# Six edits to a three-part kernel: products to GpSimd, stash copies in runs, one expert's order, weight loads on another queue

## The chip, the core and the metric

One Trainium2 chip, of which the kernel uses one core. The metric is the device time of one execution in microseconds (us). A core has TensorE (PE in the profile; its weight loads are PEld), VectorE (DVE), ScalarE (ACT), GpSimd (POOL) and SyncE (SP, here a queue for transfers only). Each engine works through its own list of instructions in order, and waits on semaphores where an instruction needs another engine's result or a transfer.

## What is computed

The reference, cut to its core. `q`, `k`, `v`, `a_re` and `a_im` are 4 x 8 x 768 x 48; `x` is 3072 x 384; there are 8 experts of 384 x 1024 x 384, and a last dense layer of 384 x 2048 x 384.

```python
# 1. a linear recurrence with a complex decay, per batch and head
scale = np.minimum(mag, 0.999) / (mag + 1e-06)
for t in range(S):
    S_re, S_im = ar * S_re - ai * S_im + kv[t], ar * S_im + ai * S_re
    y[:, :, t] = np.einsum('bhd,bhde->bhe', q[:, :, t], S_re)
# 2. of the tokens with x @ w_skip > 0 each goes to one expert
e_idx = np.argmax(xc @ w_gate, axis=1)
y[mask] = gate_w[mask, None] * (np.maximum(xc[mask] @ w1[e], 0.0) @ w2[e])
out[do_compute] = xc + y
# 3. a dense layer with a leaky ReLU
h = x @ w_in
return np.maximum(0.01 * h, h) @ w_out
```

## The kernel before

The four batches are worked in two units of two. For a unit there are these steps.

The **row side** (`attention_rows`) lays 128 rows (chunk, batch, head) on the partitions and walks through 96 time steps in blocks of 8 (at the ends fewer). Per step VectorE makes `t` (four products of the running decay product `P` with the block's normalised decay `a`) and the next `P` (two sums). Around this chain stand, per block: the normalising of `a` (`norm_pre`, `norm`: tiles `nsq`, `nr`, `nrr`, `a`) and the scaling of q and k (`scaled_pre`, `scaled`: tiles `psq`, `pg`, `pu`, `kq`). `scaled` multiplies q and k by the real and by the imaginary half of `P`; in unit 0 into `qr` and `kr`. In unit 0 `added` lets TensorE add the two squares in a bank of PSUM (tile `ad`), and `turned` transposes `qr` and `kr`, four time steps at a time, into PSUM (tile `qkps`), from where ScalarE copies them into the two `stash` tiles, which stay in SBUF and are laid out (chunk, batch and head, time). In unit 0 all of it is emitted from a table of due times (`timed`), with VectorE, ScalarE and TensorE held to that written order; `gate_products` (tiles `gv`, `gvT`, `gps`) is spread between.

The **chunk side** (`attention_chunks`) does the recurrence over eight chunks of 96 steps as matmuls. The row side of unit 1, called `behind`, runs in its gaps: `budget` lets it go on for so many microseconds of VectorE at each yield. It writes to DRAM (tile `kqd`) and not to the stash.

Then **routing**, and for the tokens of unit 0 the eight **experts** (`experts`): `gathers` fetches 128 rows for each (tile `xg`, an indirect transfer per expert), `columns` transposes them (tile `tp__`, copied by ScalarE to `xT__`), `first` and `second` are the two layers (tiles `hps`, `hh`, `yps`, `xo`), and the rows are scattered back into `xd`. The weights of unit 0's experts lie in the stash tiles in fp32; those of experts 4 to 7 are loaded by `fetch` into the place of an earlier expert's as soon as that is used. After the first layer of expert 3 `swap` lets the second stash tile go, and `convert` starts to bring `w_in` in: a 64-bit load (tile `raw`, two buffers), three VectorE instructions that put together an fp32 number (tile `cst`), a ScalarE copy to fp16 and one more VectorE instruction for the rest (tile `m2w`), 16 pieces in all. `feed` shares VectorE's budget between `behind` and this, in turns (class `share`; class `first_of` runs one to its end before the next). `BG_EXPERT` = 2.0 us are given at each of the four yields of `first`, up to expert `LASTE`.

Then the **dense** layer for unit 0's 1536 tokens: `Dense.load` (tile `xr`) reads what the experts scattered; in the first 512 tokens `w_out` is converted as well. Then unit 1: chunk side, experts (whose weights are converted to fp16 pairs), dense layer.

Which transfer stands on which queue is set in the code: nearly all on SP's, the weights of unit 0's experts on ScalarE's.

```python
    for j in range(n + 1):
        if j:
            A.activation(hi[cut(j - 1)], t[j - 1], AF.Copy, scale=scale)
        if j < n:
            r = pool.tile([128] + shape + [2], I32, tag="raw", name="raw")
            nc.sync.dma_start(...)                      # L805
```

Of the kernel before, what the change touches and what calls it, by code (L numbers as in the profile page):

```python
# [48 lines left out]
BG_START = 1.5  # L49
BG_CHUNK = 0.3  # L50
BG_ROUTE = 12.0
BG_EXPERT, LASTE = 2.0, 6
BG_DENSE = (1, 1.5, 1.5)
BG_WOUT = 0.3
BG_WSTART, BG_WEIGHT = 4.0, 0.35
# [11 lines left out]
SUM_NORM = (0, 1, 2)  # L67
SUM_SCALED = (12, 13)
MIRROR = (0, 1)
GUARD_G = (10, 11, 13)  # L70
MIRROR_G = (11, 12, 13)
LISTS = dict(sp=(0, 1), tp=(2, 3, 7), yps=(4,), ups=(5,), tr=(6,), bk=(7,))
DEEP = {"kqt": 3, "vt": 3, "qT": 3}
LISTSA = dict(sp=(0, 1), yps=(2,), ups=(3,), tr=(4, 5, 6), bk=(7,))
# [4 lines left out]
def moe_attention_kernel(ctx, tc, q, k, v, a_re, a_im, w_skip, w_gate, w1, w2, w_in, w_out, out,  # L79
# [70 lines left out]
    def rows3(x):  # L150
        return x.rearrange("(k p) f -> p k f", p=128)


    def attention_rows(ui, ep, blks, sum_pe, queue, store, stash=None, more=None):
# [124 lines left out]
        def scaled(i):  # L279
            P = Ps.pop(i)  # L280
            kq2 = ins.pop(("k", i))
            u = tl("pu", i)
            if stash:
                kq = [tl(x, i, (), (2,)) for x in ("kr", "qr")]
            else:
                kq = tl("kq", i, (), (2, 2))
                kq = [kq[:, :, a] for a in range(2)] + [kq]
            if stash:
                V.tensor_tensor(kq[1][:, :, 0], kq2[:, 1], P[:, :, 0], ALU.mult)
                yield cost(i)  # L290
                V.tensor_tensor(kq[1][:, :, 1], kq2[:, 1], P[:, :, 1], ALU.mult)
            else:
                V.tensor_tensor(kq[1], both(kq2[:, 1], i), P, ALU.mult)
            yield cost(i, 2)
            n2, g0 = pre["k", i]
            V.tensor_tensor(u, n2, g0, ALU.mult)
            yield cost(i)
            V.scalar_tensor_tensor(u, u, 2.0, g0, ALU.subtract, ALU.mult)
            yield cost(i)
            V.scalar_tensor_tensor(kq2[:, 0], kq2[:, 0], -1.0, u, ALU.mult, ALU.mult)  # L300
            yield cost(i)
            if stash:
                V.tensor_tensor(kq[0][:, :, 0], kq2[:, 0], P[:, :, 0], ALU.mult)
                yield cost(i)
                V.tensor_tensor(kq[0][:, :, 1], kq2[:, 0], P[:, :, 1], ALU.mult)
            else:
                V.tensor_tensor(kq[0], both(kq2[:, 0], i), P, ALU.mult)
            if i + 2 < nb:
                load_kq(i + 2)
            if stash:  # L310
                turns.append(turned(i, kq))
            else:
                queue.dma_start(kqd[t0s[i]:t0s[i] + blks[i]].rearrange("t r a d -> r t (a d)"),
                                kq[2].rearrange("r t a c d -> r t (a c d)"))
            yield cost(i, 2)

        def turned(i, kq):

            for g in range(0, blks[i], 4):
                m = min(4, blks[i] - g)  # L320
                for a in range(2):
                    p = ps.tile([2 * D, m, R], F32, tag="qk", name="qkps")
                    for j in range(m):
                        T.transpose(p[:, j, :], kq[a][:, g + j].rearrange("p c d -> p (c d)"), ident)
                    t = t0s[i] + g
                    lags.append((stash[a][:2 * D, :, :, t:t + m].rearrange("p c b t -> p t (c b)"), p))
                    if len(lags) > 1:
                        A.activation(*lags.pop(0), AF.Copy)
                    yield
# [461 lines left out]
    def convert(pool, src, hi, lo, scale, cut, shape, n):  # L791

        raw, t = {}, {}
        el = 1
        for d in shape:
            el *= d
        cost = (70 + 1.04 * el) / 1e3
        for j in range(n + 1):  # L800
            if j:
                A.activation(hi[cut(j - 1)], t[j - 1], AF.Copy, scale=scale)
            if j < n:
                r = pool.tile([128] + shape + [2], I32, tag="raw", name="raw")
                nc.sync.dma_start(r.rearrange("p k f w -> p k (f w)").bitcast(I64), rows3(src)[cut(j)])  # L805
                t[j] = pool.tile([128] + shape, I32, tag="cst", name="cst")
                V.tensor_scalar(t[j], r[:, :, :, 1], 0x07FFFFFF, 3, ALU.bitwise_and, ALU.logical_shift_left)
                yield 0.6 * cost
                V.scalar_tensor_tensor(t[j], r[:, :, :, 1], -0x40000000, t[j], ALU.bitwise_and, ALU.bitwise_or)
                yield cost  # L810
                V.scalar_tensor_tensor(t[j], r[:, :, :, 0], 29, t[j], ALU.logical_shift_right, ALU.bitwise_or)
                t[j] = t[j].bitcast(F32)
                yield cost
            else:
                yield 0.0
            if j:
                V.scalar_tensor_tensor(lo[cut(j - 1)], t[j - 1], scale, hi[cut(j - 1)], ALU.mult, ALU.subtract)
                yield cost
# [20 lines left out]
    class Experts:  # L839
# [2 lines left out]
            self.ui, self.whole, self.place = ui, whole, place  # L842
            self.w, self.xg, self.xt, self.h, self.slots, self.made = {}, {}, {}, {}, [], 0

        def weights(self, e, layer, half):

            src, k, m = ((w1[e], 3, F1), (w2[e], 8, DM))[layer]
            t = self.w[e, layer] = self.place(e, layer).rearrange("p (k m) -> p k m", k=k)
            c = (al, al, slice(half * m // 2, (half + 1) * m // 2)) if layer == 0 else \
                (al, slice(half * k // 2, (half + 1) * k // 2))  # L850
            nc.scalar.dma_start(t[c], rows3(src)[c])

        def part(self, i):

# [96 lines left out]
    class Dense:  # L951
# [4 lines left out]
        def load(self):  # L956
            self.xr = self.xp.tile([128, 4, DM], F32, tag="xr", name="xr", bufs=1)
            nc.sync.dma_start(self.xr, xd[self.ui][self.t * TN:(self.t + 1) * TN, :]
                              .rearrange("(s p) c -> p s c", p=128))
# [43 lines left out]
    def run(*gens):  # L1003
        for gen in gens:
            for _ in gen:
                pass
# [146 lines left out]

    def experts(ex, behind, us, then={}, mixed=none):

        ex.columns(0)
        for e in range(E):
            gen = none if ex.place else ex.made_to(2 * e + NSLOT, ex.stage)
            if e in (() if ex.place else MIX):
                next(mixed, None)  # L1160

            def go():
                for _ in range(3):
                    next(gen, None)
                budget(behind, us if e < LASTE else 0.0, "VA")

            for _ in ex.first(e):
                go()
            then.get((e, 0), list)()
            if e + 1 < E:  # L1170
                ex.columns(e + 1)
            run(gen)
            ex.second(e)
            then.get((e, 1), list)()
# [35 lines left out]
    def fetch(*which):  # L1210
        def go():
            for e, layer in which:
                for half in range(2):
                    ex.weights(e, layer, half)
        return go

    chunks_and_routing(ck[0], rt, later(BG_START, behind), BG_CHUNK,
# [12 lines left out]
    mlp2 = {}  # L1230

    def swap():
# [4 lines left out]
        for i, (shape, src, scale, cut, part) in enumerate((  # L1237
# [1 line left out]
                ([128, 16, DM], w_out, SWO, cut_rows(16, CVP), [16 // CVP, DM]))):  # L1239
            t = mlp2[i] = [wpm.tile(shape, F16, name=f"m2w{i}{j}") for j in range(2)]  # L1240
            mlp2["conv", i] = convert(cp, src, *t, scale, cut, part, CVP)
        feed.gens.append(mlp2["conv", 0])

    then = {(i // 2, i % 2): fetch((i // 2 + 2, i % 2)) for i in range(8, 12)}
    then.update({(i, 1): fetch((4 + i // 2, i % 2)) for i in range(4)})
# [196 lines left out]
```

## Time and profile before

| | |
|---|---|
| three runs | 951.84, 952.55, 953.05 us; median 952.55 |
| the profiled execution | 956.44 us, of which the span of instructions is 954.0 us |
| busy share of the span | TensorE 88%, VectorE 64%, ScalarE 54%, GpSimd 14% |
| 20 to 151 us | row side of unit 0 |
| 151 to 240 us | chunk side of unit 0 |
| 240 to 381 us | routing and experts of unit 0, conversion of `w_in` |
| 381 to 512 us | dense layer of unit 0 (its first 512 tokens up to 444, with the conversion of `w_out`) |
| 512 to 954 us | unit 1 |

A busy share is an average over stages with different limits, so each stage has to be read by itself. The profile names the line of a helper (L91) for all compute instructions, so tiles tell them apart. "a <-b" is an output and its inputs; a wait is put down to what came last.

### The profile page before, as it was taken

To read this page: it belongs to the slowest core of one execution; us is meant where nothing else is said; L and a number is where in the kernel's file an instruction comes from. 1 tells how busy PE (TensorE), PEld (TensorE's weight loads), DVE (VectorE), ACT (ScalarE), POOL (GpSimd) and SP (SyncE) were. 2 spreads that over 40 slices of the span, in tenths; PEclk is the share of its full clock that TensorE was granted. 3 is DMA by queue.
4 is the path that set the end of the run, shared out by engine and by line. 5 is a ranking of instruction groups with operands and counts; after the bars stand their busy time and mean duration, and the time that the engine had idled before them with its cause. 6 is when DMAs were issued, how large, how long until landed. Compare 5 with 4: busy or idle time off the path is not lost.

```text
span 954.0 us, 17829 instructions
## 1 busy us (share of the span) xinstructions
PE 840.4 (88%) x6674; PEld 584.8 (61%) x6674; DVE 612.4 (64%) x1534; ACT 518.0 (54%) x1065; POOL 137.2 (14%) x168
## 2 busy tenths in 40 slices
PE   1787878899299783999999988999999999999997
PEld 1665667898288572455457978846776645546454
DVE  6978884677788579999961555587577262260430
ACT  4879896676255343654743867655566261350430
POOL 9100022221541012000012111140011000000000
PEclk9979897999599986999999989999999999999999
DMA  5555544898668876445246898242766201000000
GB/s 152 143 152 159 139 114 144 243 290 268 200 206 276 283 271 217 147 134 172 78 156 165 224 234 241 75 162 86 246 201 214 88 1 51 18 1 25 9 10 27
DMA packets 126512, 143.61 MB, mean 151 GB/s; under 512 B 34058, under 2 KB 109514, under 8 KB 126416
## 3 DMA queue, kind: packets, MB, share of 16 engines
q1 hardware_dynamic: 106064, 107.88, 38.5%
q10 hardware_dynamic: 18304, 29.89, 9.6%
q0 software_dynamic: 2048, 4.61, 1.4%
q8 instruction: 54, 0.88, 0.4%
q14 instruction: 42, 0.34, 0.1%
HBM read 115.62 MB, written 28.41 MB: 151 GB/s over the span
## 4 chain that ended last, share of the span: by engine, by line
PE 55%; DVE 16%; DMA 14%; ACT 10%; issue 3%; SPq 1%; ACTq 0%; POOL 0%; DVEq 0%; POOLq 0%
PE ops L91 17%; PE hps L91 13%; PE yps L91 7%; PE sps L91 4%; DVE gg L91 3%; DMA raw<-in_moe_w_in_dram 3%; DVE gl L91 3%; DVE cst L91 2%; PE ad L91 2%; ACT stash L91 2%; PE tps L91 2%; ACT gh L91 2%; DMA kqt<-kqd 2%; PE ups L91 2%; DMA cw<-in_moe_w_dram 2%
## 5 line engine op out<-in xcount | busy, mean ns | idle before, releaser
L91 PE MATMUL hps<-xTh,m2w 128*128 128x512 f16 x576 | 174.1, 381 | 0.6 <-issue 0.3
L91 PEld LDWEIGHTS <-m2w 128*128 128x128 f16 x864 | 84.5, 98 | 100.7 <-issue 3.9
L91 PE MATMUL ops<-m2w,gh 128*128 128x384 f16 x512 | 125.2, 326 | 0.0
L91 PE MATMUL hps<-xTl,m2w 128*128 128x512 f16 x288 | 109.4, 381 | 0.1
L91 DVE TENSOR_TENSOR gg<-hps,gg 128x512 f32<-128x512 f32 x96 | 65.8, 685 | 65.5 <-ACT gg L91 65.1
L91 PE MATMUL ops<-m2w,gl 128*128 128x384 f16 x256 | 83.5, 326 | 0.0
L91 ACT ACTIVATE ot<-ops 128x384 f32<-128x384 f32 x24 | 11.6, 489 | 121.2 <-PE ops L91 121.2
L91 PEld LDWEIGHTS <-gh 128*128 128x128 f16 x512 | 50.1, 98 | 32.7
L91 DVE TENSOR_TENSOR t<-P,a 128x192 f32<-128x192 f32 x190 | 66.8, 352 | 1.3 <-ACT a L91 0.4
L91 PE MATMUL ops<-m2w,stash 128*128 128x384 f16 x384 | 65.3, 326 | 1.8 <-ACT m2w L91 1.8
L91 ACT ACTIVATE gg<-hps 128x512 f32<-128x512 f32 x96 | 56.3, 586 | 17.5 <-PE hps L91 12.4
L91 DVE TENSOR_TENSOR gl<-gg,gh 128x512 f16<-128x512 f32 x64 | 44.2, 690 | 33.6 <-ACT gh L91 33.3
L91 DVE SCALAR_TENSOR_TENSOR w<-cw,w 128x768 f16<-128x768 f32 x64 | 59.8, 953 | 7.7 <-ACT w L91 7.2
L91 ACT ACTIVATE gh<-gg 128x512 f16<-128x512 f32 x64 | 40.3, 630 | 43.2 <-DVE gg L91 42.9
L91 ACT ACTIVATE w<-cw 128x768 f16<-128x768 f32 x64 | 53.0, 844 | 17.9 <-DMA cw<-in_moe_w_dram 15.4
L91 POOL TENSOR_SCALAR_AFFINE_SELECT sc<-sc 96x384 f32<-96x384 f32 x64 | 34.6, 550 | 157.6 <-ACT sc L91 157.2
L91 PEld LDWEIGHTS <-stash 128*128 128x128 f16 x384 | 37.5, 98 | 29.2 <-issue 4.8
L91 POOL DMA_INDIRECT xd<-xo,idx x16 | 25.2, 1574 | 179.9 <-DVE xo L91 166.1
L91 ACT ACTIVATE stash<-qkps 96x512 f32<-96x512 f32 (+1 forms) x50 | 50.0, 1025 | 0.4 <-PE qkps L91 0.4
L91 DVE TENSOR_TENSOR P<-t 128x96 f32<-128x96 f32 x190 | 48.5, 255 | 1.6
L91 PE MATMUL yps<-stash,hh 128*128 128x384 f32 x128 | 44.7, 503 | 3.8 <-ACT hh L91 3.8
L91 ACT ACTIVATE hh<-hps 128x256 f32<-128x256 f32 (+1 forms) x64 | 23.8, 378 | 40.6 <-PE hps L91 28.7
(245 smaller groups left out, 1779.6 us busy)
## 6 DMA issues: line engine op xcount, KB each, us to landing
stash<-in_moe_w_dram ACTq DMA_DIRECT2D x32, 768.0 KB
cw<-in_moe_w_dram SPq DMA_DIRECT2D x64, 384.0 KB
kqt<-kqd SPq DMA_DIRECT2D x16, 576.0 KB
kqd<-kq SPq DMA_DIRECT2D x14, 576.0 KB
vd<-gv SPq DMA_DIRECT2D x32, 192.0 KB
vt<-vd SPq DMA_DIRECT2D x32, 192.0 KB
raw<-in_moe_w_in_dram SPq DMA_DIRECT2D x16, 384.0 KB
raw<-in_moe_w_out_dram SPq DMA_DIRECT2D x16, 384.0 KB
```

The source lines that it names most:

```text
L91: ins = getattr(self.engine, op)(*args, **kw)
```

## The change

It has six parts. The two products of `scaled` with q are made by GpSimd in blocks 0 to 10 of unit 0 (`SCALED_G`), and six smaller instructions of blocks 10, 11 and 13 that GpSimd made (`GUARD_G`, `MIRROR_G`) go back to ScalarE. The copy into the stash runs over four time steps innermost. In `experts` of unit 0 TensorE is held to the written order up to the second expert's transposes. `convert` asks for its next piece one piece ahead, and its first as soon as `swap` runs. `feed` gives the conversion all of VectorE's budget until it is done, and then `behind`; and expert 6 has the budget as well (`LASTE` = 7). `fetch` puts the weights of experts 4 to 7 on SP's queue.

```diff
-BG_EXPERT, LASTE = 2.0, 6
+BG_EXPERT, LASTE = 2.0, 7
...
-GUARD_G = (10, 11, 13)
-MIRROR_G = (11, 12, 13)
+GUARD_G = ()
+MIRROR_G = ()
+SCALED_G = range(11)
...
             if stash:
-                V.tensor_tensor(kq[1][:, :, 0], kq2[:, 1], P[:, :, 0], ALU.mult)
+                X = G if i in SCALED_G else V
+                X.tensor_tensor(kq[1][:, :, 0], kq2[:, 1], P[:, :, 0], ALU.mult)
                 yield cost(i)
-                V.tensor_tensor(kq[1][:, :, 1], kq2[:, 1], P[:, :, 1], ALU.mult)
+                X.tensor_tensor(kq[1][:, :, 1], kq2[:, 1], P[:, :, 1], ALU.mult)
...
-                    lags.append((stash[a][:2 * D, :, :, t:t + m].rearrange("p c b t -> p t (c b)"), p))
+                    lags.append((stash[a][:2 * D, :, :, t:t + m].rearrange("p c b t -> p (c b) t"),
+                                 p.rearrange("p t r -> p r t")))
...
+        def load(j):
+            raw[j] = pool.tile([128] + shape + [2], I32, tag="raw", name="raw")
+            nc.sync.dma_start(raw[j].rearrange("p k f w -> p k (f w)").bitcast(I64), rows3(src)[cut(j)])
+
+        load(0)
+        yield 0.0
         for j in range(n + 1):
+            if j + 1 < n:
+                load(j + 1)
             if j:
                 A.activation(hi[cut(j - 1)], t[j - 1], AF.Copy, scale=scale)
             if j < n:
-                r = pool.tile([128] + shape + [2], I32, tag="raw", name="raw")
-                nc.sync.dma_start(r.rearrange("p k f w -> p k (f w)").bitcast(I64), rows3(src)[cut(j)])
+                r = raw.pop(j)
...
-        def weights(self, e, layer, half):
+        def weights(self, e, layer, half, queue=nc.scalar):
...
-            nc.scalar.dma_start(t[c], rows3(src)[c])
+            queue.dma_start(t[c], rows3(src)[c])
...
+        if ex.place:
+            keep("T")
         ex.columns(0)
         for e in range(E):
...
             if e + 1 < E:
                 ex.columns(e + 1)
+            keep("")
             run(gen)
...
-                    ex.weights(e, layer, half)
+                    ex.weights(e, layer, half, nc.sync)
...
-        feed.gens.append(mlp2["conv", 0])
+        next(mlp2["conv", 0])
+        feed.gens = [first_of([mlp2["conv", 0]] + feed.gens)]
```

VectorE's list in the row side of unit 0, in the middle of a block (`qr<-kq_566` are the two products with q of the block before), first as it was:

```order
L91 TENSOR_TENSOR P<-t_774 128x96
L91 TENSOR_TENSOR qr<-kq_566,P 128x8x48
L91 TENSOR_TENSOR t_787<-P,a_614 128x192
L91 TENSOR_TENSOR qr<-kq_566,P 128x8x48
L91 TENSOR_TENSOR P<-t_787 128x96
L91 TENSOR_TENSOR t_802<-P,a_614 128x192
```

and the same place with the change:

```order
L92 TENSOR_TENSOR P<-t_774 128x96
L92 TENSOR_TENSOR t_787<-P,a_614 128x192
L92 TENSOR_TENSOR P<-t_787 128x96
L92 TENSOR_TENSOR t_802<-P,a_614 128x192
L92 TENSOR_TENSOR P<-t_802 128x96
```

The two products have left VectorE's list, and the chain's rows close up. GpSimd's list with the change, from its last memsets of the start on:

```order
L92 MEMSET gv_153 96x8x16
L92 MEMSET stash 32x12288 x2
L92 TENSOR_TENSOR qr<-kq_109,P 128x4x48 x2
L92 TENSOR_TENSOR qr<-kq_115,P 128x8x48 x2
L92 TENSOR_TENSOR qr<-kq_305,P 128x8x48 x2
```

The products stand there one block after the other, behind the stash's memset.

TensorE's list where the experts of unit 0 begin (`tp__3514` and `tp__3610` are the transposed rows of the first and of the second expert), as it was:

```order
L91 MATMUL bank<-incl_1_3334,ones 96x8
L91 MATMUL tp__3514<-ident,xg_3474 128x128 x3
L91 MATMUL tp__3610<-ident,xg_3479 128x128 x3
L91 MATMUL hps<-xT__3518,stash 128x128 x24
L91 MATMUL yps_3616<-stash,hh 128x384 x8
```

and with the change:

```order
L92 MATMUL bank<-incl_1_3334,ones 96x8
L92 MATMUL tp__3514<-ident,xg_3474 128x128 x3
L92 MATMUL hps<-xT__3518,stash 128x128 x24
L92 MATMUL tp__3610<-ident,xg_3479 128x128 x3
L92 MATMUL yps_3616<-stash,hh 128x384 x8
```

The second expert's transposes went behind the first expert's first layer. SP's queue in the later experts (`raw` are the pieces of `w_in`, `ari` and `kq` belong to `behind`, each with the semaphores that it waits for), as it was:

```order
L805 DMA raw<-in_moe_w_in_dram 128x3x128 [waits DMAHW5_49,DVE_49]
L805 DMA raw<-in_moe_w_in_dram 128x3x128 [waits DMAHW7_49,DVE_49]
L201 DMA ari<-in_a_re_dram 128x1x288 [waits DMAHW0_49,DVE_49,Activation_49]
L202 DMA ari<-in_a_im_dram 128x1x288 [waits DMAHW1_49]
L805 DMA raw<-in_moe_w_in_dram 128x3x128 [waits DMAHW5_49,DMAHW3_49,DVE_49]
```

and with the change (`stash<-in_moe_w_dram` are weights of experts 6 and 7):

```order
L805 DMA raw<-in_moe_w_in_dram 128x3x128 [waits DMAHW5_49,DVE_49]
L805 DMA raw<-in_moe_w_in_dram 128x3x128 [waits DMAHW6_49,DVE_49]
L861 DMA stash<-in_moe_w_dram 128x3x512 [waits DMAHW7_49,PE_49]
L861 DMA stash<-in_moe_w_dram 128x3x512 [waits DMAHW0_49,PE_49]
L805 DMA raw<-in_moe_w_in_dram 128x3x128 [waits DMAHW5_49,DMAHW1_49,DVE_49]
L805 DMA raw<-in_moe_w_in_dram 128x3x128 [waits DMAHW6_49,DMAHW2_49,DVE_49]
L861 DMA stash<-in_moe_w_dram 128x4x384 [waits DMAHW3_49,PE_49]
L861 DMA stash<-in_moe_w_dram 128x4x384 [waits DMAHW4_49,PE_49]
```

Pairs of pieces and pairs of weight loads now take turns on the one queue, and the weights there wait for TensorE.

## Rows read from the trace of the kernel before

**Rows 1.** Windows view, six stretches: busy time (count) per engine, granted clock, DMA share, GB/s.
```profile
20.00:140.00 120.00, 97.52 (x626) 74.18 (x627) 101.67 (x308) 102.48 (x207) 13.58 (x7) 0.89 0.54 145
...
140.00:151.00 11.00, 6.68 (x41) 4.51 (x39) 7.34 (x28) 10.58 (x22) 2.88 (x5) 0.78 0.30 86
...
262.00:307.00 45.00, 45.00 (x269) 36.52 (x268) 36.96 (x107) 24.75 (x64) 14.40 (x9) 0.96 0.73 236
...
307.00:381.00 74.00, 49.98 (x272) 39.29 (x271) 55.05 (x140) 29.47 (x73) 10.74 (x11) 0.84 0.80 259
...
381.00:444.00 63.00, 60.74 (x298) 29.70 (x296) 60.28 (x132) 35.39 (x69) 0.00 (x0) 0.97 0.46 145
...
444.00:512.00 68.00, 68.00 (x386) 37.56 (x384) 49.06 (x130) 32.62 (x75) 6.82 (x9) 1.00 0.49 145
```

**Rows 2.** Chain of waits from 20 to 151 us, its shares by engine and line.
```profile
by line: PE ad L91 17.2%; ACT stash L91 16.6%; issue 8.7%; PE gps L91 8.5%; ACT psq L91 8.5%; ACT gvT L91 5.6%; PE gtps L91 5.6%; ACT nsq L91 4.1%; DMA ari<-in_a_im_dram 3.2%; ACT a L91 3.1%; PE qkps L91 2.9%; ACT gv L91 2.5%; DVE t L91 2.0
```

**Rows 3.** VectorE groups from 20 to 151 us: busy, mean ns, idle before and its releaser.
```profile
L91 DVE TENSOR_TENSOR qr<-kq,P 128x384 f32<-128x384 f32 x20 | 11.0, 551 | 0.0
...
L91 DVE TENSOR_TENSOR pu<-ad,pg 128x384 f32<-128x384 f32 x10 | 5.6, 559 | 14.6 <-ACT pg L91 14.6
```

**Rows 4.** Groups of the whole run, shapes kept apart: ScalarE, VectorE, GpSimd.
```profile
L91 ACT ACTIVATE stash<-qkps 96x512 f32<-96x512 f32 x46 | 47.9, 1062 | 0.0
...
L91 ACT ACTIVATE sT<-stp 96x512 f32<-96x512 f32 x28 | 16.6, 593 | 2.9 <-PE stp L91 2.7
...
L91 DVE TENSOR_REDUCE LG<-xps 96x9 f32<-96x72 f32 x32 | 7.3, 228 | 47.5 <-ACT xrow L91 47.3
...
L91 DVE TENSOR_REDUCE em<-cand 96x14 f32<-96x112 f32 x2 | 0.5, 266 | 0.1
...
L91 POOL TENSOR_SCALAR_AFFINE_SELECT sc<-sc 96x384 f32<-96x384 f32 x64 | 34.6, 550 | 157.6 <-ACT sc L91 157.2
```

**Rows 5.** Timeline: GpSimd beside VectorE: start us, length us, instruction.
```profile
128.16 2.55 POOL L91 TENSOR_SCALAR a<-a 128x192 f32<-128x192 f32 x1 [7.59 <-DVE a L91]
...
128.53 0.25 DVE L91 TENSOR_TENSOR P<-t 128x96 f32<-128x96 f32 x1
...
186.94 1.67 POOL L91 TENSOR_SCALAR_AFFINE_SELECT sc<-sc 96x384 f32<-96x384 f32 x2 [3.12 <-ACT sc L91]
...
188.11 0.61 DVE L91 TENSOR_TENSOR P<-t 128x96 f32<-128x96 f32 x1
```

**Rows 6.** Timeline: one block's last product on VectorE, and TensorE's first transposes of it.
```profile
63.90 0.55 DVE L91 TENSOR_TENSOR qr<-kq,P 128x384 f32<-128x384 f32 x1
...
72.11 0.60 PE L91 MATMUL qkps<-ident,qr 128*96 128x128 f32 x4
```

**Rows 7.** Timeline from 254 to 262 us: the first two experts on TensorE and ScalarE.
```profile
255.11 0.49 ACT L91 ACTIVATE xT__3518<-tp__3514 128x384 f32<-128x384 f32 x1 [1.58 <-PE tp__3514 L91]
...
260.89 0.90 PE L91 MATMUL tp__3610<-ident,xg 128*128 128x128 f32 x3 [5.82 <-DMA xg<-xd,idx]
...
261.58 0.64 PE L91 MATMUL hps<-xT__3518,stash 128*128 128x128 f32 x2
```

**Rows 8.** Chain of waits from 307 to 381 us, in order of time: start us, us, what.
```profile
310.52 9.57 DMA raw<-in_moe_w_in_dram
...
372.00 7.22 DMA xr<-xd
```

**Rows 9.** Waits from 307 to 381 us: us in total, times, longest us.
```profile
DVE cst L91 <- DMA raw<-in_moe_w_in_dram: 13.2, 9, 5.8
...
PE hps L91 <- ACT xT__4174 L91: 4.9, 1, 4.9
...
PE yps L91 <- ACT hh L91: 3.8, 2, 3.0
```

**Rows 10.** Timeline: DMA issues on ScalarE's queue (ACTq).
```profile
317.28 4.03 ACTq L851 DMA_DIRECT2D stash<-in_moe_w_dram  x2
...
334.26 5.35 ACTq L851 DMA_DIRECT2D stash<-in_moe_w_dram  x2
```

## The prediction

> **What bounds the kernel now.** I read the windows view first, stage by stage, then in each stage that the change touches the chain of waits, the groups and the timeline.
>
> In the row side of unit 0 no engine is full, and three are nearly so: from 20 to 140 us TensorE is busy for 97.5 of 120 us, VectorE for 101.7, ScalarE for 102.5 [rows 1]. The chain goes to and fro between TensorE and ScalarE; the stash copies are its largest piece that isn't TensorE's, with 16.6% of 131 us, or 21.7 us [rows 2]. VectorE stands behind them: its idle time before `pu` ends with ScalarE's `pg`, 14.6 us in ten blocks [rows 3]. From 140 to 151 us ScalarE alone is full (10.58 of 11), nearly all of it stash copies [rows 1].
>
> The experts of unit 0 are two stages. From 262 to 307 us TensorE is busy throughout [rows 1], so what starts it earlier counts in full. From 307 to 381 us nothing is full: TensorE is busy for 50.0 of 74 us, VectorE for 55.1 [rows 1]. The chain there goes through transfers: a piece of `w_in` takes 9.57 us from issue to landing, and the rows for the dense layer (`xr`) 7.22 us at the end [rows 8]. VectorE waits 13.2 us for pieces [rows 9].
>
> From 381 to 444 us VectorE is the bound (60.3 of 63 us), from 444 to 512 us TensorE (68 of 68) [rows 1]. What `behind` and the conversions still owe VectorE at 381 is paid in the first of the two; the second has 19 us of VectorE to spare. Unit 1 is not touched.
>
> **The change part by part.**
>
> *Stash copies.* 46 copies of 512 columns take 1.062 us each. Another ScalarE copy of 512 columns out of PSUM, `sT`, takes 0.593 us; it writes its columns one after the other, where the stash copy scatters them singly [rows 4]. The change writes runs of four and reads PSUM with a stride instead. No ScalarE row reads so. The nearest is VectorE's sum `LG`, which reads single numbers 64 apart in PSUM: 72 of them in 0.228 us, against 0.266 us for the 112 of `em` side by side in SBUF [rows 4], which is no sign of a price. So I take 0.6 us a copy, with 1.06 us as the other end (the stride costs in reading what it cost in writing). That is 46 x 0.46 = 21 us less of ScalarE.
>
> *Six instructions back to ScalarE*, of 384 columns at most. Each is less than the 0.593 us of `sT`; at 0.4 us they make +2.4 us.
>
> *Products to GpSimd.* 22 instructions leave VectorE; the 20 of 384 columns in [rows 3] are 11.0 us, two of them stay, and the first block's two are shorter, so some 10.5 us leave it. GpSimd's length for such a product is in no row. Its select over 384 columns, with one input, takes 0.55 us [rows 4]; twice that, 1.1 us, for two inputs is my value. The other end is 2.55 us, which a smaller instruction took while VectorE worked without a gap [rows 5]. Two a block make 2.2 to 5.1 us. They have 8.2 us, from the start of VectorE's last product at 63.90 to TensorE's first transposes of it at 72.11 [rows 6], so they aren't late. If that cover were gone, TensorE and then ScalarE would stop behind them in order. The first block's pair stands behind the stash's memset and is the one place where I leave a delay open.
>
> They do cost VectorE something. In [rows 5] a `P` that starts inside a GpSimd select takes 0.61 us, where the one at 128.53 takes 0.25 us: 0.36 us held by one instruction with one input. With two inputs I take 0.7 us; 22 x 0.7 = 15 us, against 10.5 us taken away. The difference of 5 us goes into VectorE's 18 us of idle time of [rows 1].
>
> The Trainium skill speaks against this edit: by SBUF — State Buffer, "Who interferes with whom", a VectorE instruction with two SBUF inputs and a GpSimd instruction that reads SBUF exclude one another, for the length of one. The row agrees that VectorE is held, for 0.36 us of 0.55. By GPSIMD Engine Reference, "Elementwise — side-by-side cycle accounting", a two-input instruction takes about 2.6 cycles an element, which gives an estimate of 0.83 us for 384; 22 of those would be 18 us on VectorE, and the sum for it +8 us rather than +5. No run so far shows such a product.
>
> What the row side gains by all three: of 21.7 us of copies on the chain 44% goes, 9.5 us. The next chains are near (VectorE at 85% of the stretch plus 5 us, TensorE at 81%), and the six instructions stand on it too. But from 140 to 151 us ScalarE's gain is whole, with seven or eight copies. I take **-8 us**; ends +2.5 (copies no faster) and -14.
>
> *The first expert's order.* The first layer of expert 0 can start when `xT__3518` is copied: 255.11 + 0.49 = 255.6 us. It starts at 261.58, since the second expert's transposes stand ahead and wait until 260.89 for their gather [rows 7]. With the order written out it starts **5.9 us** earlier; the gather is there before the first layer ends. TensorE's 45 full us [rows 1] hand that on to 307.
>
> *Weights on SP's queue, pieces ahead, conversion first.* ScalarE stands 4.03 and 5.35 us at issues of weights [rows 10], and TensorE waits 4.9 and 3.8 us for ScalarE [rows 9]. These 8.7 us go, but TensorE has 24 us of idle time in this stage, so alone they are worth nothing. What counts is VectorE's 19 us of idle time there. 13.2 us of it is waiting for pieces. Asking earlier, in pairs, with the row side to fill in, should take two thirds of that, -9.5 us. I don't take all, since the pieces now queue with the weights on SP, which wait for TensorE. In VectorE's list two more steps of the row side than before stand ahead of the end of `w_out`'s conversion; at 101.7 us for ten blocks of eight steps [rows 1, 3] that is 1.3 us each, +2.5 us. Sum **-7 us**; ends +2.5 and -14. `LASTE` = 7 puts 8 us more of VectorE's work before the last expert's rows; it hides in the same idle time, and if that is gone, `xr` is late by it.
>
> The sum is -8 - 5.9 - 7 = -20.9 us, against the profiled execution's 956.4 us: 935.5. That execution is 3.9 us above the median, so I forecast 931.6, say **932 us**.
>
> **The rivals.**
> 1. *The copies don't get faster.* For it: no row shows a strided read by ScalarE. Against: [rows 4]. The first term goes to +1, the sum to -12: 941 us.
> 2. *The later experts gain nothing.* Pieces at 9.57 us a landing, with the transfers at 0.80 of their time [rows 1, 8], set the conversion's pace, and the 5.9 us are waited away there too. For it: that share, and three things on one queue. Only the row side is left: 944.5 us.
> 3. *SP's queue becomes the chain.* Weights wait on it for TensorE, and pieces behind them. Seven pairs, each with 9.57 us to land and 2.2 us for four VectorE instructions of at most 0.55 us [rows 3, 8], are 82 us from 302: 384 us, and `xr` then at 391 against 379. With the row side's -8 that is +4: 957 us. It decides from a landing of 9.2 us a pair on. Against: with two buffers the landings overlap VectorE's work, and 9.57 us was seen in a crowd only.
> 4. *Slower, by GpSimd.* A product holds VectorE for all of the 2.55 us of [rows 5]: 22 x 2.55 = 56 us, less 10.5 and 18 of idle time, +28; with the other terms +15: 967 us. It decides from 1.9 us a product. Against: at 128.16 GpSimd waited, and the `P` inside its 2.55 us took its usual 0.25 us [rows 5].
> 5. *The terms cancel*, about 951 us.
>
> **How the numbers follow.** Chances: forecast 0.53 (own range 922 to 941), rivals 0.15, 0.17, 0.06, 0.05, 0.04. Faster by more than 0.2% (1.9 us, about what a measurement of this kernel can tell): 0.53 + 0.15 + 0.17 = 0.85; within it 0.04; slower 0.11. The range takes in rivals 1 and 2 and leaves out the rest at both ends: 920 to 950.
>
> **What would show it.** Right: stash copies near 0.6 us; the last of them about 8 us earlier; `hps` of expert 0 right behind its `xT__`, before `tp__` of expert 1; no issue on ScalarE's queue over 1 us in the later experts; less than 5 us of waits for `w_in` pieces; the dense layer's first matmul 18 to 25 us earlier. Wrong: copies still at 1 us; `P` and `t` that take twice their time beside `qr` on GpSimd; TensorE waiting for `qr`; SP's queue standing at weights while VectorE waits for pieces; the gain of the experts given back before 444.

## The result, and the profile after

Four runs took 920.58 to 928.26 us, median 925.17, against 952.58 before: a ratio of 0.9709 (95% interval 0.9663 to 0.9755), by the ratio 27.7 us less. Measured once more the ratio was 0.9719 (0.9689 to 0.9750). The forecast was 932 us, 20.6 us less.

The profiled execution took 920.58 us with a span of 918.9. Set against the profiled one of before, at the points where the stages begin:

| start of | before, us | after, us | earlier by | in this stage |
|---|---|---|---|---|
| chunk side (first `sps`) | 153.55 | 138.69 | 14.9 | 14.9 |
| first layer of expert 0 | 261.58 | 241.39 | 20.2 | 5.3 |
| first `cst` of `w_in` | 308.67 | 289.06 | 19.6 | -0.6 |
| dense layer (first `hps` of `xTh`) | 381.06 | 350.17 | 30.9 | 11.3 |
| end of the span | 954.0 | 918.9 | 35.1 | 4.2 |

The last 4.2 us are in stages that the change hardly touches: the profiled execution of before is 3.9 us above its median and that of after 4.6 below. So 30.9 us is what the traces give the change up to there, where the sum of the prediction had 20.9; how much of the chance difference of the two executions lies in the 30.9 can't be told.

The windows view of after, the stages that answer to [rows 1]; its columns are those of [rows 1].

```profile
20.00:134.00 114.00, 95.42 (x660) 71.56 (x659) 111.47 (x309) 94.16 (x229) 33.77 (x28) 0.96 0.57 158
...
134.00:145.00 11.00, 9.86 (x88) 9.03 (x88) 2.40 (x8) 4.78 (x12) 2.61 (x6) 0.69 0.38 108
...
251.00:290.00 39.00, 39.00 (x236) 30.89 (x235) 35.64 (x103) 25.02 (x64) 9.76 (x6) 1.00 0.85 280
...
290.00:350.00 60.00, 42.92 (x255) 33.74 (x254) 54.62 (x142) 26.99 (x66) 27.34 (x11) 0.89 0.88 296
...
350.00:413.00 63.00, 60.83 (x302) 30.14 (x301) 61.13 (x134) 36.11 (x70) 0.00 (x0) 0.97 0.54 171
...
413.00:480.00 67.00, 67.00 (x380) 36.99 (x379) 44.17 (x116) 30.05 (x65) 6.82 (x9) 1.00 0.45 132
```

VectorE, not ScalarE, is full in the row side now: 111.5 of 114 us, where [rows 1] had 101.7 of 120; ScalarE went from 102.5 of 120 to 94.2 of 114. The 11 us in which ScalarE alone was full (10.58 of 11) have ScalarE at 4.78. The later experts (290 to 350) take 60 us in place of 74. From 350 on the two stages are about as long as before.

The groups view of after, 0 to 140 us, shapes kept apart; the columns are those of [rows 3].

```profile
L92 ACT ACTIVATE stash<-qkps 96x512 f32<-96x512 f32 x46 | 26.5, 584 | 0.0
...
L92 POOL TENSOR_TENSOR qr<-kq,P 128x384 f32<-128x384 f32 x20 | 23.3, 1185 | 66.4 <-DVE P L92 33.6 <-PE gtps L92 15.5 <-DMA kq<-in_q_dram 9.6
...
L92 DVE SCALAR_TENSOR_TENSOR nrr<-nrr,nr 128x384 f32<-128x384 f32 x10 | 10.3, 1032 | 0.0
...
L92 DVE TENSOR_TENSOR P<-t 128x96 f32<-128x96 f32 x95 | 28.9, 304 | 1.4
...
L92 DVE TENSOR_TENSOR pu<-ad,pg 128x384 f32<-128x384 f32 x10 | 5.5, 549 | 0.0
```

The stash copy takes 0.584 us (1.062 in [rows 4]). A product on GpSimd takes 1.185 us; 1.1 was assumed. VectorE's wait for `pg` before `pu`, 14.6 us in [rows 3], is gone. But `nrr<-nrr,nr` has 1.032 us, where other instructions of that shape have 0.55, and `P` has 0.304 in place of 0.25. The timeline shows why:

```profile
65.56 2.35 POOL L92 TENSOR_TENSOR qr<-kq,P 128x384 f32<-128x384 f32 x2 [7.73 <-PE gtps L92]
...
65.72 0.35 DVE L92 TENSOR_TENSOR t<-P,a 128x192 f32<-128x192 f32 x1
...
65.99 0.55 DVE L92 TENSOR_TENSOR nrr<-ad,nrr 128x384 f32<-128x384 f32 x1
...
66.46 0.60 DVE L92 TENSOR_TENSOR P<-t 128x96 f32<-128x96 f32 x1
...
66.98 1.35 DVE L92 SCALAR_TENSOR_TENSOR nrr<-nrr,nr 128x384 f32<-128x384 f32 x1
```

While GpSimd makes its two products (65.56 to 67.91), `t` and then `nrr<-ad,nrr`, which reads `ad` from PSUM, keep their 0.35 and 0.55 us; `P` takes 0.60 and the next `nrr`, with both inputs in SBUF, 1.35: together 1.15 us more than usual for two products.

TensorE's timeline at the first experts, which answers to [rows 7]:

```profile
239.93 0.88 PE L92 MATMUL tp__3514<-ident,xg 128*128 128x128 f32 x3 [5.87 <-DVE nrr L92]
...
241.39 8.51 PE L92 MATMUL hps<-xT__3518,stash 128*128 128x128 f32 x48 [0.58 <-ACT xT__3518 L92]
...
249.73 0.49 PE L92 MATMUL tp__3610<-ident,xg 128*128 128x128 f32 x3
```

The first layer of expert 0 begins 1.46 us after its transposes, where it was 7.38, and the second expert's transposes no longer stand before it. The waits view of after from 290 to 350 us, which answers to [rows 9]:

```profile
DVE cst L92 <- DMA raw<-in_moe_w_in_dram: 3.7, 4, 1.6
...
PE yps L92 <- ACT hh L92: 0.8, 1, 0.8
...
PE tp L92 <- DMA xr<-xd: 16.2, 1, 16.2
```

VectorE's waits for pieces went from 13.2 to 3.7 us (6.0 us in after2, the second trace of the same kernel), TensorE's for ScalarE from 8.7 to 0.8. What TensorE has left there is one wait of 16.2 us for `xr`.

### The profile page after: what moved, and what is told of

The parts are those of the page before. It is cut to its first block, busy times and chain, and to the rows that moved or that the text cites. A ratio compares the mean times of both kernels' runs of the same rounds, so it can differ in the third digit from the quotient of the medians.

```text
span 918.9 us, 17853 instructions
## 1 busy us (share of the span) xinstructions
PE 824.7 (90%) x6674; PEld 573.5 (62%) x6674; DVE 614.7 (67%) x1512; ACT 502.6 (55%) x1071; POOL 171.1 (19%) x184
## 4 chain that ended last, share of the span: by engine, by line
PE 50%; DVE 23%; DMA 14%; ACT 8%; issue 3%; SPq 1%; ACTq 0%; DVEq 0%; POOLq 0%; POOL 0%
PE ops L92 18%; PE hps L92 12%; PE yps L92 6%; DVE gg L92 4%; PE sps L92 3%; DMA raw<-in_moe_w_in_dram 3%; DVE cst L92 3%; DMA stash<-in_moe_w_dram 3%; DVE gl L92 3%; PE tps L92 2%; ACT gh L92 2%; DVE t L92 2%; PE ad L92 2%; DMA cw<-in_moe_w_dram 2%; DMA kqt<-kqd 2%
## 5 line engine op out<-in xcount | busy, mean ns | idle before, releaser
L92 POOL DMA_INDIRECT xd<-xo,idx x16 | 40.6, 2536 | 148.2 <-DVE xo L92 109.5
L92 DVE TENSOR_TENSOR P<-t 128x96 f32<-128x96 f32 x190 | 52.7, 277 | 1.8
L92 PE MATMUL ad<-psq,ident 128*128 128x384 f32 (+2 forms) x48 | 23.1, 617 | 20.9 <-ACT psq L92 20.9
L92 PE MATMUL yps<-sc,vt 128*64 128x96 f32 x512 | 41.6, 251 | 0.0
```

The costliest lines, as they stand in the source:

```text
L92: ins = getattr(self.engine, op)(*args, **kw)
```

## The experiments

Three sets of four kernels, each set on one chip beside the kernel before: p_runs to p_conv; after2 to m_feed; p_sp, x1, x2 and x4. Differences in us are the ratio times the 952.6 us of before. Two marks in the traces were read for all: the start of the chunk side, which ends the row side, and the stretch from the first layer of expert 0 to the dense layer's first matmul (119.5 us before; kernels with the first expert's order begin it before the second expert's gather is there, so their measure is p_first's 121.9).

| kernel | what it is | ratio (95% interval) | us | chunk side starts | stretch |
|---|---|---|---|---|---|
| p_runs | before + copies in runs | 0.9852 (0.9813 to 0.9892) | -14.1 | 136.95 | 118.9 |
| p_qr | before + products on GpSimd | 1.0048 (1.0003 to 1.0092) | +4.6 | 157.28 | 121.9 |
| p_first | before + first expert's order | 0.9946 (0.9918 to 0.9975) | -5.1 | 151.00 | 121.9 |
| p_conv | before + conversion's part | 0.9897 (0.9862 to 0.9931) | -9.8 | 153.91 | 108.7 |
| p_sp | before + weights on SP's queue | 0.9876 (0.9828 to 0.9923) | -11.8 | 153.91 | 108.4 |
| after2 | the change | 0.9719 (0.9689 to 0.9750) | -26.8 | 141.03 | 107.5 |
| m_qr | change, products on VectorE | 0.9683 (0.9654 to 0.9712) | -30.2 | 137.85 | 109.6 |
| m_queue | change, weights on ScalarE's queue | 0.9887 (0.9854 to 0.9920) | -10.8 | 140.64 | 129.6 |
| m_feed | change, conversion in turns | 0.9668 (0.9628 to 0.9708) | -31.6 | 138.88 | 105.5 |
| x1 | m_qr and m_feed together | 0.9662 (0.9623 to 0.9700) | -32.2 | 141.69 | 105.6 |
| x2 | x1, no asking ahead | 0.9732 (0.9698 to 0.9767) | -25.5 | 137.62 | 107.9 |
| x4 | x1, `BG_EXPERT` 1.6 | 0.9700 (0.9662 to 0.9738) | -28.6 | 142.26 | 105.1 |

**The row side.** p_runs has the copies alone:

```diff
-  lags.append((stash[a][:2 * D, :, :, t:t + m].rearrange("p c b t -> p t (c b)"), p))
+  lags.append((stash[a][:2 * D, :, :, t:t + m].rearrange("p c b t -> p (c b) t"),
+               p.rearrange("p t r -> p r t")))
```

> The kernel before with the stash copies in runs of four and nothing else. Theory A (the copies alone were the row side's chain; the products only move the same hold from VectorE's list into its instructions): the copies take 0.58 us as in the changed kernel, the row side ends 12 to 15 us earlier, the time falls by as much, to 938 to 941 us. Rival B (with ScalarE relieved VectorE with its products is the next bound, and both parts are needed): the row side gains 8 us or less, 944 us or more. In both VectorE's instructions keep their lengths (nrr 0.55, P 0.25 us).

p_qr has the products alone, with the six small instructions back on ScalarE:

```diff
-GUARD_G = (10, 11, 13)
-MIRROR_G = (11, 12, 13)
+GUARD_G = ()
+MIRROR_G = ()
+SCALED_G = range(11)
```

> The kernel before with the products with q on GpSimd and the six small instructions back on ScalarE, nothing else. Theory A: ScalarE stays the chain and gets 2.4 us more, VectorE is held for 11 us in all for the 11 us taken from it: the time stays within 2 us of 952.5 or rises to 955.5. Rival B (VectorE was the chain beside ScalarE, and its 11 us count): 944 to 949 us.

p_runs gave 14.1 us, the whole of the row side's gain: theory A, though in its trace the chunk side starts 16.6 us earlier, a little more than A allowed. Its groups view, 20 to 150 us:

```profile
L91 ACT ACTIVATE stash<-qkps 96x512 f32<-96x512 f32 x46 | 26.6, 585 | 0.1
...
L91 DVE TENSOR_TENSOR pu<-ad,pg 128x384 f32<-128x384 f32 x10 | 5.6, 555 | 2.4 <-ACT pg L91 2.4
...
L91 DVE SCALAR_TENSOR_TENSOR nrr<-nrr,nr 128x384 f32<-128x384 f32 x8 | 4.4, 555 | 0.0
```

VectorE keeps its products here, its instructions have their usual lengths, and its wait for `pg` still falls from 14.6 to 2.4 us. p_qr lost 4.6 us (0.3 to 8.8), in the middle more than the 3 us that theory A allowed for, and rival B fell. How much of it is the products' and how much the six instructions' on ScalarE isn't separated. Its groups view, the same stretch:

```profile
L92 DVE TENSOR_TENSOR t<-P,a 128x192 f32<-128x192 f32 x88 | 36.4, 414 | 0.8
...
L92 DVE TENSOR_TENSOR P<-t 128x96 f32<-128x96 f32 x89 | 28.5, 320 | 1.4
...
L92 DVE TENSOR_TENSOR pu<-ad,pg 128x384 f32<-128x384 f32 x10 | 5.5, 554 | 7.9 <-ACT pg L92 7.9
```

The hold falls on `t` (0.414 in place of 0.352) and `P` (0.320 in place of 0.254): 88 x 62 ns + 89 x 66 ns = 11.3 us. The same comparison with before gives 2.4 us more on `nrr<-nrr,nsq` and 1.9 on `a`: 15.6 us in all, 0.71 us a product, against 11.7 us of products that left (20 of 384 columns, 11.0 us, and two of 192).

m_qr puts the products of the changed kernel back on VectorE (`SCALED_G = ()`), beside after2:

> The changed kernel again, as the measure for the three beside it on the same chip. A ratio of 0.966 to 0.976 to the kernel before, as in the first measurement.

> The changed kernel with all products with q on VectorE (the six small instructions stay on ScalarE). Theory A (GpSimd's products hold VectorE for as much as they take from it, and in its full list the hold counts): VectorE's nrr goes from 1.03 back to 0.55 us and P from 0.30 to 0.25, the first sps starts 1 to 3 us earlier, the time is 1 to 4 us below the changed kernel's. Rival B (with VectorE full the 11 us taken from its list are worth it): the row side ends 3 to 10 us later, and the time is as much above.

after2 is as expected. m_qr came out 3.4 us below it, with intervals that overlap. But both intervals carry the spread of the same runs of before; set against each other, all six times of m_qr (923.52 to 925.58) lie below all six of after2 (926.58 to 930.00), 2.6 us by the medians, and `nrr` and `P` are back at 0.552 and 0.254 us. So theory A is borne out on this chip. The same edit between m_feed and x1, on two chips, makes 0.6 us, and the start of the chunk side doesn't show where a gain would lie: it is at 138.69, 141.03, 140.64 and 138.88 us in the four kernels with runs and products on GpSimd, mean 139.8, and 137.85, 141.69, 137.62 and 142.26 in the four with runs and products on VectorE, mean 139.9 (136.95 in p_runs, where the six small instructions are still GpSimd's). Nothing is gained by the products; that they cost 2 to 3 us is likely, and not shown in the stage where they are. Rival B, 3 to 10 us lost, fell.

**The first expert's order.**

```diff
+        if ex.place:
+            keep("T")
         ex.columns(0)
...
+            keep("")
             run(gen)
```

> The kernel before with TensorE held to the written order for the first expert, nothing else. Theory A (TensorE full from there to the fifth expert, and what starts it earlier counts to the end): 5.9 us less, 946 to 947.5 us. Rival B (the later experts wait for pieces of w_in and for weights at a pace of their own and eat it): 951 to 953 us, with VectorE's waits for pieces up by as much as the first layer of expert 0 is earlier.

5.1 us: theory A within its interval (2.4 to 7.8 us). In the profile the dense layer starts 4.8 us earlier than before, though the first layer starts 7.1 us earlier, 1.2 of it since its transposes came earlier: part of the gain is waited away on the way (the stretch is 121.9 us in place of 119.5). By the waits view 1.2 us of that is TensorE's waits for `hh` (5.0 us for 3.8) and 0.8 its wait for `xr` (16.2 for 15.4). Rival B's mark, VectorE's waits for pieces, is 14.0 us, only 0.8 more than before.

**The later experts.** p_conv has the whole part (pieces ahead, conversion first, `LASTE` 7, queue), p_sp one argument of it:

```diff
-                    ex.weights(e, layer, half)
+                    ex.weights(e, layer, half, nc.sync)
```

> The kernel before with the conversion's part alone: pieces asked for ahead, conversion before the row side of unit 1, LASTE 7, weights of experts 4 to 7 on SP's queue. Theory A (the gain in the later experts stands by itself): the stretch from the first cst to the dense layer's first matmul is 9 to 12 us shorter, as in the changed kernel, and the time is 940.5 to 943.5 us. Rival B (it is worth so much only because the experts begin earlier and nothing of it stands alone): 947 us or more.

> The kernel before with the weights of experts 4 to 7 on SP's queue and nothing else. Theory A (the prediction: the issues on ScalarE's queue stand beside idle time of TensorE, so the queue alone is worth nothing): 0.998 to 1.002 of the kernel before. Rival B (on ScalarE's queue the weights set how far the conversion runs ahead in ScalarE's and VectorE's lists and how long these stand at pieces; that is the gain of the later experts): 6 to 14 us less, 0.985 to 0.994, with ScalarE's waits for cst in the later experts down from 22.3 us to about 11.

For p_conv theory A holds: the part stands by itself, with 9.8 us (and 10.3 us less between the first `cst` and the dense layer). But p_sp has 11.8 us with the queue alone; the stretch is 108.7 and 108.4 us. So p_sp's theory A fell. Its rival B is right on the size, and its mark failed: ScalarE's waits for `cst` stay, at 23.4 us. What went is TensorE's waits behind ScalarE, seen on ScalarE's timeline of the kernel before (ACTq are issues of transfers), and on TensorE's:

```profile
333.13 0.52 ACT L91 ACTIVATE m2w<-cst 128x384 f16<-128x384 f32 x1 [5.56 <-DVE cst L91]
...
334.19 0.49 ACT L91 ACTIVATE xT__4174<-tp__4170 128x384 f32<-128x384 f32 x1 [0.53 <-issue]
...
334.26 5.35 ACTq L851 DMA_DIRECT2D stash<-in_moe_w_dram  x2
...
339.72 0.39 ACT L91 ACTIVATE hh<-hps 128x256 f32<-128x256 f32 x1 [5.04 <-DMA stash<-in_moe_w_dram]
...
354.10 0.99 ACT L91 ACTIVATE m2w<-cst 128x384 f16<-128x384 f32 x2 [6.65 <-DVE cst L91]
```

```profile
329.37 0.49 PE L91 MATMUL tp__4225<-ident,xg 128*128 128x128 f32 x3
...
334.73 8.52 PE L91 MATMUL hps<-xT__4174,stash 128*128 128x128 f32 x48 [4.87 <-ACT xT__4174 L91]
...
356.74 7.12 PE L91 MATMUL yps<-stash,hh 128*128 128x384 f32 x16 [2.98 <-ACT hh L91]
```

The transposed rows `tp__4225` are those of the last expert; the expert before it waits for `xT__4174`. Its copy stands on ScalarE behind the `m2w` at 333.13, which waited 5.56 us for a piece, and behind an issue, which added 0.53 us. TensorE's other long wait, 2.98 us for an `hh` at 356.74, comes behind the `m2w` pair at 354.10, which had waited 6.65 us. The issue of 5.35 us makes one `hh` 5.04 us late, but TensorE is at work on `hps` then and goes on to `yps` without a wait; nor does a wait of TensorE follow the issue of 4.03 us [rows 10]. So the long waits come from `m2w` copies that stand ahead in ScalarE's list and wait for pieces; that the two long issues cost TensorE anything isn't shown.

With the weights gone from ScalarE's list its order is another. Counted on the timelines, five `m2w` stand ahead of the copy of expert 6's rows in before, p_runs, p_qr and p_first, and all four have TensorE's wait for that copy, 4.4 to 4.9 us. Three stand there in p_sp and x2, four in p_conv, after, after2, m_feed, x1 and x4, and none of these has it; m_queue, further on, has eight and a wait of 3.8 us. No kernel changed this order alone, so that it is the cause is argued. TensorE's timeline in the same place of p_sp:

```profile
323.95 5.33 PE L91 MATMUL yps<-stash,hh 128*128 128x384 f32 x16
...
329.12 5.52 PE L91 MATMUL hps<-xT__4174,stash 128*128 128x128 f32 x48
...
334.80 5.33 PE L91 MATMUL yps<-stash,hh 128*128 128x384 f32 x16
```

First and second layers follow each other without a gap, and 48 matmuls take 5.52 us where the kernel before had 8.52. The windows view of that stretch, and then of the whole stage from the first `cst` to the dense layer, of before and then of p_sp, has the other part of it, the clock:

```profile
329.00:343.00 14.00, 9.13 (x53) 8.66 (x52) 11.50 (x31) 2.55 (x6) 1.72 (x1) 0.76 0.71 246
...
308.67:381.06 72.39, 48.37 (x257) 37.62 (x256) 53.55 (x138) 28.11 (x70) 10.59 (x11) 0.84 0.79 259
```

```profile
329.00:343.00 14.00, 14.00 (x96) 11.69 (x95) 12.98 (x34) 5.80 (x15) 4.35 (x1) 1.00 0.87 296
...
308.42:371.08 62.66, 44.29 (x266) 34.94 (x265) 49.49 (x128) 26.82 (x65) 17.44 (x11) 0.87 0.90 288
```

Granted 0.76 of full speed before, after 4.87 us of standing, and 1.00 in p_sp. The stage is 9.7 us shorter: TensorE is busy for 4.1 us less with the same layers (48.37 and 44.29) and idle for 5.6 us less (24.0 and 18.4). And TensorE's idle time at the end of this stage, in the waits of before and of p_sp:

```profile
PE tp L91 <- DMA xr<-xd: 15.4, 1, 15.4
```

```profile
PE tp L91 <- DMA xr<-xd: 17.7, 1, 17.7
...
PE yps L91 <- ACT hh L91: 0.7, 1, 0.7
...
ACT m2w L91 <- DVE cst L91: 23.4, 12, 4.0
...
DVE cst L91 <- DMA raw<-in_moe_w_in_dram: 7.3, 7, 3.5
```

It stays, at 15.4 and 17.7 us: it comes after the last expert, in series. VectorE's waits for pieces went from 13.2 to 7.3 us with the queue alone.

m_queue and m_feed take one thing each out of the changed kernel: the queue, and the conversion's place ahead of the row side (`feed.gens.append` again).

> The changed kernel with the weights of experts 4 to 7 back on ScalarE's queue. VectorE's list changes with it: 157 steps of the row side stand ahead of the end of the second conversion in place of 168. Theory A (what VectorE has to do before the dense layer decides, the queue doesn't): 11 steps of 1.3 us less of it, of which TensorE's and the transfers' own work leaves about half: 5 to 10 us below the changed kernel. Rival B (ScalarE stands at the issues again for 4 to 5 us each, and TensorE and the conversion wait for it): 4 to 9 us above the changed kernel.

> The changed kernel with the conversion and the row side of unit 1 in turns again, as before; pieces are still asked for ahead. Theory A (asking ahead is the gain, the turns only share out the same work): within 2 us of the changed kernel; VectorE's waits for pieces stay under 5 us. Rival B (the turns put the conversion behind row side steps, and the dense layer waits for its last pieces): 4 to 9 us above, with the first matmul of the dense layer later by as much.

m_queue gave back 16 us of 27 (0.9887 beside 0.9719). Theory A fell altogether. Rival B had the direction and at most little more than half of the size, and its reason failed: the 16 issues are back on ScalarE's queue, and none stands longer than 1.02 us. The stretch, 129.6 us, is longer than in the kernel before. Its waits from 262 to 381 us:

```profile
ACT m2w L92 <- DVE cst L92: 46.6, 18, 11.6
...
DVE cst L92 <- DMA raw<-in_moe_w_in_dram: 24.0, 9, 8.8
...
PE hps L92 <- ACT xT__4062 L92: 7.8, 1, 7.8
```

and one such place on VectorE, ScalarE (with its longest issue) and TensorE:

```profile
304.84 0.36 DVE L92 TENSOR_SCALAR cst<-raw 128x384 int32<-128x384 int32 x1 [8.83 <-DMA raw<-in_moe_w_in_dram]
```

```profile
277.50 1.02 ACTq L861 DMA_DIRECT2D stash<-in_moe_w_dram  x2
...
307.01 0.52 ACT L92 ACTIVATE m2w<-cst 128x384 f16<-128x384 f32 x1 [11.64 <-DVE cst L92]
...
307.44 0.47 ACT L92 ACTIVATE xT__4062<-tp__4058 128x384 f32<-128x384 f32 x1
```

```profile
307.96 4.42 PE L92 MATMUL hps<-xT__4062,stash 128*128 128x128 f32 x19 [7.83 <-ACT xT__4062 L92]
```

A piece is 8.83 us late; the `m2w` copy that needs it holds ScalarE for 11.64 us, and behind it stands `xT__4062`, the copy of expert 5's rows, for which TensorE waits 7.83 us. Three `m2w` stand ahead of that copy here, two in every other kernel. In VectorE's list 17 pieces of the conversions stand ahead of the last expert's output here, 13 in the changed kernel: with the weights off SP's queue the planned order runs the conversion further ahead than its pieces land. That this order is the whole cause is argued from the trace; no kernel changed the order alone.

m_feed came out 5 us below after2 (0.9668 beside 0.9719, the intervals overlap), with a stretch of 105.5 us against 107.5 and 108.8 in the two traces of the change. Rival B fell; the conversion's place is not a gain. Theory A missed too, in the time and in its mark: VectorE's waits for pieces are 10.3 us, more than in after2 (6.0), and yet the kernel isn't slower.

**Versions.** Beside each other:

> The changed kernel with two edits undone, GpSimd's products and the conversion ahead of the row side. Theory A (both cost by themselves, 2.6 and 5 us in the two single runs, in different stages): 0.961 to 0.966 of the kernel before. Rival B (the two single differences were chance of a few us): 0.969 to 0.973, as the changed kernel.

> As x1, with the pieces asked for one by one as before too, so that of the conversion's part only LASTE 7 and the queue are left. Theory A (the prediction: asking ahead takes away VectorE's waits for pieces, and that is the gain of the later experts): 5 to 10 us above x1, VectorE's waits for pieces back at 13 us or more. Rival B (the queue is the gain): within 2 us of x1.

> As x1, with 1.6 us in place of 2.0 for the row side and the conversion at each yield of an expert, which puts five steps of the row side behind the second conversion (158 in place of 163). Theory A (VectorE is full from 350 to 413 us and has 11 us of idle time from 413 to 480, so steps moved across are free): 2 to 6 us below x1. Rival B (TensorE's work and the transfers set this stretch): within 2 us of x1, or above it where the last steps aren't covered.

x1 has the lowest ratio of all, 0.9662 (0.9623 to 0.9700), just outside theory A's range; the gain over the change is some 5 us, with intervals that still touch. It is hardly lower than m_feed (0.9668, on another chip), so the products on VectorE add nothing to it that can be told. x2, without asking ahead, is 6.7 us above x1 (theory A; the intervals just touch). VectorE's waits from 262 to 381 us, of x2 and then of x1:

```profile
DVE cst L92 <- DMA raw<-in_moe_w_in_dram: 16.1, 7, 5.9
```

```profile
DVE cst L92 <- DMA raw<-in_moe_w_in_dram: 8.7, 7, 3.0
```

VectorE's waits for pieces are 16.1 us in x2 and 8.7 in x1. Only 2.2 us of the difference lie in the stretch, and the spans of the two profiled executions are only 2.7 us apart, so the traces don't place the rest. x2 holds little more than the three edits that gained alone, 14.1 + 5.1 + 11.8 = 31.0 us, and gains 25.5: they don't quite add up. `LASTE` 7 and the six instructions on ScalarE are in it too, and neither was tried alone.

x4 is not faster than x1, so its theory A fell. The dense layer starts 4.3 us later in x4's trace, so its window is shifted by as much; the windows of x4 and then of x1:

```profile
417.30:484.30 67.00, 65.17 (x369) 35.93 (x368) 63.27 (x171) 39.55 (x89) 0.30 (x1) 1.00 0.43 134
```

```profile
413.00:480.00 67.00, 64.50 (x364) 35.52 (x364) 56.59 (x152) 35.66 (x79) 6.59 (x9) 1.00 0.44 137
```

VectorE's idle time there is 3.7 us in x4 and 10.4 in x1: the steps did move into it, as meant. But the stretch of the experts is only 0.5 us shorter for it (105.1 and 105.6), as in rival B.

## Why the prediction was right, and where it was off

The direction and the range were right, and each of the three gains was there; the sum was 10 us short in the trace and 7 in the measurement.

**Row side, -8 forecast.** The copies came out as taken (0.584 us for 0.6) and so, nearly, did GpSimd's products (1.185 for 1.1, and for the 0.83 us of the other estimate). The size was off: "44% of 21.7 us goes, 9.5 us", less the six instructions and the hold. Measured were 14.1 us by p_runs and 13.3 as the mean of the eight traces above against the four of before with slow copies (153.55, 151.00, 153.91, 153.91, mean 153.1). ScalarE's whole 21 us were not to be had, since VectorE became nearly full (in p_runs too, with 108.0 of 114 us), but taking the copies' share of the chain was too little: of VectorE's 14.6 us of waits for ScalarE [rows 3] p_runs gave back 12.2, and the copies behind 140 us are shorter besides. Why the share was too small is argued only: `ad` and `psq` of [rows 2] stand in lists behind copies, and a chain names what ran last.

**Products to GpSimd.** The net cost was forecast as VectorE's +5 us into idle time: 0.7 us of hold for each of 22, less the 10.5 us that leave. That of the 20 of 384 columns "two of them stay" was a misreading: all 20 left, so it is 11.7 us. The hold was 0.71 us a product in p_qr, which makes +3.9 us. With the copies in runs it is 12.5 us in after (10 x 0.48 us on `nrr`, 95 x 0.05 on `P`, the rest on `t` and smaller shapes) and 13.9 in after2, both against m_qr's lengths, or +1 to +2 us. The idle time into which it was to go was gone by then. p_qr lost 4.6 us, the six instructions included; with fast copies it is 2.6 us or less. The rule that spoke against the edit (the Trainium skill, SBUF — State Buffer, "Who interferes with whom") has the direction: `P` and `nrr` at 66.46 and 66.98, each with two SBUF inputs, are held, and the one that reads PSUM isn't. `t` at 65.72 has two as well and isn't, but in p_qr `t` is held too. The hold of this pair is 1.15 us of 2.35, not the whole.

**First expert, -5.9.** Right: the first layer comes 5.92 us sooner behind its transposes, 5.1 us in p_first.

**Later experts, -7.** This step failed in its reasons, though its size was near (-11 in the trace, within its ends). "These 8.7 us go, but TensorE has 24 us of idle time in this stage, so alone they are worth nothing": p_sp gives 11.8 us with the queue alone. The 24 us are 15.4 us after the last expert, for `xr`, and the 8.7 us themselves; the tail didn't cover the waits, it came behind them, and TensorE's layers, at the lower clock after them, took 4.1 us longer besides. The waits were also put beside the wrong thing, the issues of 4.03 and 5.35 us: they come behind `m2w` copies that wait for pieces, and m_queue loses 16 us with no issue over 1.02 us. "What counts is VectorE's 19 us of idle time" fell too: p_conv, with pieces ahead and all, is no better than p_sp, and m_feed waits longer for pieces than after2 and isn't slower. That asking ahead gains something and the conversion's place takes it back (x2 +6.7, m_feed -5) rests on intervals that touch or overlap. Rival 3, SP's queue as the chain, didn't come: with the weights on SP's queue TensorE's waits behind ScalarE's list went away. The Trainium skill (DMA: Bandwidth & Descriptors, "Issuing engines are not separate DMA queues") says that starting transfers from several engines saves only the time in which the sequencer starts them, usually small beside the transfer. Here the choice of the engine was worth 11.8 us, and the traces point to the order of ScalarE's list for it, not to the issues' own time.

## What to carry to other kernels

Before idle time of an engine is counted as slack, look at where in the stage it lies: waits in the middle and a tail in series at the end are both on the path. When one engine's work shrinks, look at the waits for it on the next engine: here these 14.6 us were nearer to the gain of 14.1 than the 9.5 us by its share of the chain. What stands ahead in an engine's list counts as much as its own length: `m2w` copies that waited for late pieces held the copies behind them, and with these TensorE. A transfer's issue stands in that list too, and moving issues to another queue can change the order of all that is left.

## What was not expected of the hardware

ScalarE's copy that reads PSUM with a stride and writes runs of four (0.584 us) costs no more than the plain one of 512 columns (0.593 us in [rows 4]). The hold by GpSimd isn't spread evenly: the pair of products shown, of 2.35 us, held VectorE for 1.15 us, all of it on the two instructions that began in its last 1.5 us; over a whole row side `nrr` and `P` bear most of it in the change, `t` and `P` in p_qr. And four kernels with the same row side ended it up to 4.6 us apart (137.62 to 142.26), as much as several of the differences that were looked for.
